# Another written-out order for a fused linear-attention and squared-ReLU kernel

## The chip, the cores and the metric

The kernel runs on one core of one Trainium2 chip. The metric is the device time of one execution in microseconds, as a median over runs. A smaller number is better.

## The reference

Two layers follow each other. The first is a linear attention with a decaying state, for 4 batches, 8 heads, 768 positions and a head width of 48; the second is a feed-forward block with a squared ReLU, on 3072 tokens of width 384 and a hidden width of 2048.

```python
for t in range(S):
    cur = einsum('bhd,bhe->bhde', u * k[t], v[t])
    y[t] = einsum('bhd,bhde->bhe', r[t], state + cur)
    state = w[None, :, :, None] * state + einsum('bhd,bhe->bhde', k[t], v[t])
x = y.transpose(0, 2, 1, 3).reshape(B * S, H * D)
h = np.maximum(x @ w_in, 0.0)
out = (h * h) @ w_out
```

Inputs and output are float32. TensorE works on bfloat16 copies of them.

## The kernel before

**Units.** The 768 positions are cut into 6 chunks of 128. A unit is one chunk of one batch, so there are 24 units; unit `i` belongs to chunk `i // 4` and batch `i % 4`. A unit's attention goes through these steps, each a Python function of the kernel:

- `load` brings the unit's k, r or v from memory (192 KB each, three DMAs per unit). `scale:i:1` multiplies k by a power of the decay, `scale:i:0` multiplies r, both on VectorE into the tile `rkw`. `cast_v` makes the bfloat16 copy of v on ScalarE.
- `turn` (TensorE transposes, for units 0 to 5, copied out of PSUM by ScalarE's `evict_rk`) or `turn_dma` (a DMA transpose on SyncE's queue, for units 6 to 23) gives `rkT`. `rk` multiplies its halves on VectorE.
- `at` (or `ats` for two units at once) computes the attention scores on TensorE; `mask` evicts them on VectorE in two halves (`mask:i:0`, `mask:i:1`) into `am`. `sums` computes the diagonal and the state's increment; `state_add`, `state_decay` (VectorE) and `state_cast` (ScalarE) carry the state on.
- `y_mm` computes the unit's y on TensorE; `diag_v` and `evict_y` on VectorE add the diagonal part and write `yb`. `x_turn` and `evict_x` (units 0 to 5) or a DMA transpose `x_dma` on SyncE's queue (units 6 to 23) give `xT`, the input of the feed-forward block.

**The feed-forward block.** `mm1:i:m:s` multiplies `xT` of `m` units (one at a time in the first two chunks, two at a time later) by a slice `s` of w_in. `relu` evicts it on ScalarE into `gr`; `square` makes `g` either on ScalarE (`...:1`) or on VectorE (`...:0`). `mm2:i:q` multiplies a quarter of the hidden width by w_out into a bank that stays open over q = 0 to 3; `evict_o` on ScalarE and `store` bring the result out. The last unit's product is done in two halves (`mm2_half`, `evict_half`, `store_half`).

**The order.** Nothing is left to a scheduler. The table `SCHEDULE` holds all words in one list, and each engine executes its own words in the list's order; the engines meet only through the waits that the data need. `load:3:kt:POOL` names the queue that issues a DMA (SyncE's or GpSimd's). The numbers behind `@` are the PSUM banks of the word, out of eight: a word that takes a bank waits until whoever read the bank's last content is done. `fill` is a matmul on constants whose result nobody reads; it stands only in the first part of the list.

```python
for word in SCHEDULE.split():
    times, _, word = word.rpartition("*")
    word, _, taken = word.partition("@")
    name, *args = word.split(":")
    for _ in range(int(times or 1)):
        given[:] = [int(x) for x in taken.split(",") if x]
        steps[name](*[value(x) for x in args])
```

In the profile's rows, lines of the kernel stand for these words: L232 `fill`, L236 `spread_log`, L287 `scale`, L301 `turn_dma`, L310 `turn`, L314 `evict_rk`, L319 `rk`, L327 `at`/`ats`, L339 `mask`, L347 and L352 `sums`, L361 `diag_v`, L390 and L396 `y_mm`, L405 `evict_y`, L414 `x_dma`, L420 `x_turn`, L424 `evict_x`, L434 `mm1`, L442 `relu`, L451 and L453 `square`, L460 `mm2`, L467 `evict_o`, L475 `mm2_half`.

## Time and profile before

| | us |
|---|---|
| median of 3 runs (lowest, highest) | 174.15 (173.06, 174.81) |
| the profiled execution | 172.5 |
| its span, from the first to the last instruction | 170.4 |
| TensorE busy in the span | 163.4 |
| VectorE busy | 137.0 |
| ScalarE busy | 120.9 |
| GpSimd busy | 30.5 |

The span is what the trace shows; 2.1 us of the profiled execution lie around it. That execution is 1.65 us shorter than the median of the runs without a profile, and the runs themselves lie 1.75 us apart. Busy time of TensorE contains the constant matmuls of `fill`, and its instructions are pipelined, so that the times of two neighbours overlap: the distance from one start to the next tells what a matmul costs.

### The profile page before, as it was taken

How to read it: one execution, taken by the hardware profiler on the slowest of the kernel's cores; microseconds unless marked ns; L12 is line 12 of the kernel's file. 1: busy time of each engine (PE TensorE's matmuls, PEld its weight loads, DVE VectorE, ACT ScalarE, POOL GpSimd, SP SyncE). 2: the span in 40 equal slices, each digit the busy share in tenths (PEclk: the TensorE clock that was granted, in tenths of full speed). 3: DMA queues.
4: the chain of work that ended last, by engine and by line, in shares of the span. 5: the costliest groups of instructions: out<-in, count | busy, mean ns of one | idle time of the engine just before them, and what ended most of it. 6: DMA issues, size and time to landing. Idle time of an engine off the chain costs nothing.

```text
span 170.4 us, 4781 instructions
## 1 busy us (share of the span) xinstructions
PE 163.4 (96%) x1917; PEld 129.9 (76%) x1917; DVE 137.0 (80%) x297; ACT 120.9 (71%) x253; POOL 30.5 (18%) x62
## 2 busy tenths in 40 slices
PE   3899999999999999999999999999999999999993
PEld 2467998778778786795796895896898776999662
DVE  5359969969998999799988979988999898664800
ACT  3355489997685988579499499599359985295830
POOL 7989540000000500001100001203000030030010
PEclk9999999999999999999999999999999999999999
DMA  6999999989999999998999994998989994150014
GB/s 115 188 220 211 221 248 244 227 155 129 187 159 187 209 237 133 192 207 131 250 203 116 200 217 81 251 192 176 252 100 212 197 159 139 27 162 0 4 63 167
DMA packets 94784, 28.83 MB, mean 169 GB/s; under 512 B 90665, under 2 KB 92714, under 8 KB 94762
## 3 DMA queue, kind: packets, MB, share of 16 engines
q1 hardware_dynamic: 90512, 19.08, 73.9%
q0 software_dynamic: 4224, 9.44, 21.4%
q8 instruction: 15, 0.25, 0.6%
q14 instruction: 7, 0.06, 0.2%
q10 hardware_dynamic: 26, 0.00, 0.0%
HBM read 20.45 MB, written 4.72 MB: 148 GB/s over the span
## 4 chain that ended last, share of the span: by engine, by line
PE 84%; DVE 6%; DMA 5%; issue 1%; ACT 1%; ACTq 1%; DVEq 0%
PE bank L434 35%; PE bank L460 31%; PE bank L327 4%; DMA xT<-yb 3%; PE bank L390 3%; DMA rkT<-rkw 2%; PE bank L352 2%; PE bank L232 2%; PE bank L396 2%; PE bank L310 2%; PE bank L475 2%; DVE am L339 1%; DVE rkw L287 1%; PE bank L347 1%; DVE g L453 1%
## 5 line engine op out<-in xcount | busy, mean ns | idle before, releaser
L442 ACT ACTIVATE gr<-bank 128x512 f32<-128x512 f32 x96 | 53.1, 603 | 27.3 <-PE bank L434 25.9
L434 PE MATMUL bank<-xT,w_in_q 128*128 128x128 bf16 (+1 forms) x768 | 70.8, 246 | 0.6 <-DMA xT<-yb 0.4
L460 PE MATMUL bank<-w_out_q,g 128*128 128x384 bf16 x368 | 68.1, 327 | 0.1
L434 PEld LDWEIGHTS <-w_in_q 128*128 128x128 bf16 x768 | 64.2, 113 | 3.4 <-DMA xT<-yb 0.5
L460 PEld LDWEIGHTS <-g 128*128 128x128 bf16 x368 | 33.7, 98 | 19.2 <-DVE g L453 0.6
L453 DVE TENSOR_TENSOR g<-gr 128x512 bf16<-128x512 f32 x49 | 32.4, 686 | 6.9 <-ACT gr L442 6.8
L494 POOL DMA_DIRECT2D out_dram<-osb x21 | 11.3, 543 | 129.4 <-ACT osb L467 118.7
L339 DVE TENSOR_TENSOR am<-bank,smask 128x512 bf16<-128x512 f32 x48 | 31.4, 685 | 2.9 <-PE bank L327 2.8
L451 ACT ACTIVATE g<-gr 128x512 bf16<-128x512 f32 x47 | 29.1, 638 | 0.6
L287 DVE TENSOR_TENSOR rkw<-ldk,wneg 128x384 bf16<-128x384 f32 x24 | 13.2, 553 | 4.8 <-ACT wneg L240 3.6
L381 ACT CAST stb<-st 64x192 bf16<-64x192 f32 x40 | 13.9, 348 | 2.6 <-DVE st L375 2.3
L361 DVE TENSOR_TENSOR dv<-vb,bank 128x384 f32<-128x384 bf16 x24 | 13.0, 550 | 2.4 <-PE bank L352 1.5
L405 DVE TENSOR_TENSOR yb<-bank,dv 128x384 bf16<-128x384 f32 x24 | 13.3, 555 | 1.3 <-PE bank L396 0.3
L287 DVE TENSOR_TENSOR rkw<-ldr,wpos 128x384 bf16<-128x384 f32 x24 | 13.1, 553 | 1.0 <-DMA ldr<-in_r_dram 0.8
L319 DVE TENSOR_TENSOR rk<-rkT 128x512 bf16<-128x512 bf16 x24 | 10.0, 420 | 3.8 <-ACT rkT L314 2.0
L467 ACT COPY osb<-bank 128x384 f32<-128x384 f32 x23 | 10.5, 483 | 2.7 <-PE bank L460 2.7
L291 ACT CAST vb<-ldv 128x384 bf16<-128x384 f32 x24 | 12.1, 512 | 0.4 <-DMA ldv<-in_v_dram 0.3
L371 DVE TENSOR_TENSOR st<-bank,st 64x192 f32<-64x192 f32 x32 | 11.2, 351 | 1.2 <-PE bank L352 0.9
L232 PE MATMUL bank<-warm 128*128 128x256 bf16 x39 | 9.2, 334 | 2.0 <-DVE warm L183 1.5
L314 ACT COPY rkT<-bank 128x512 bf16<-128x512 bf16 x12 | 6.9, 595 | 3.7 <-PE bank L310 3.6
L390 PEld LDWEIGHTS <-am 128*128 128x128 bf16 x192 | 7.9, 96 | 2.0 <-issue 0.7
L327 PEld LDWEIGHTS <-rkT 64*128 64x128 bf16 x192 | 5.5, 96 | 4.2 <-issue 3.9
(58 smaller groups left out, 112.2 us busy)
## 6 DMA issues: line engine op xcount, KB each, us to landing
ldk<-in_k_dram SPq DMA_DIRECT2D x22, 192.0 KB, 4.6
out_dram<-osb POOLq DMA_DIRECT2D x21, 192.0 KB, 3.3
ldr<-in_r_dram SPq DMA_DIRECT2D x20, 192.0 KB, 3.7
ldv<-in_v_dram SPq DMA_DIRECT2D x19, 192.0 KB, 4.3
w_in_q<-in_moe_w_in_dram POOLq DMA_DIRECT2D x4, 384.0 KB, 8.9
w_out_q<-in_moe_w_out_dram POOLq DMA_DIRECT2D x4, 384.0 KB, 10.7
ldv<-in_v_dram POOLq DMA_DIRECT2D x5, 192.0 KB, 9.0
ldr<-in_r_dram POOLq DMA_DIRECT2D x4, 192.0 KB, 8.2
```

Source lines behind the costliest of these rows:

```text
L232: nc.tensor.matmul(out=banks[given.pop(0)][:, :n], lhsT=warm[:, :128], rhs=warm[:, :n], start=True, stop=True)
L287: nc.vector.tensor_tensor(t["rkw"][:, x, :, :, :D], pair(src), pair(wx), ALU.mult)
L339: nc.vector.tensor_tensor(am, t["at"][o], smask.unsqueeze(1).to_broadcast([C, HP, C]), ALU.mult)
L361: nc.vector.tensor_tensor(t["dv"], t["vb"], t["d"].unsqueeze(2).to_broadcast([C, H, D]), ALU.mult)
L381: nc.scalar.copy(stb[b][sl, :, o * D : (o + 1) * D], st32[b][sl])
L390: nc.tensor.matmul(out=y[:, 2 * p + o, :], lhsT=t[f"am{o}"][:, p, :], rhs=t["vb"][:, 2 * p + o, :], start=(o == 0 and p == 0), stop=c == 0 ...
L405: nc.vector.tensor_tensor(t["yb"], t["y"], t["dv"].rearrange("p h d -> p (h d)"), ALU.add)
L434: nc.tensor.matmul(out=t["h", s][:, a], lhsT=turned, rhs=chunks[c]["xT"][:, n, b : b + m, :], start=(n == 0), stop=(n == NK - 1),)
L442: nc.scalar.activation(t["gr", s], t["h", s], AF.Relu)
L451: nc.scalar.activation(g, x, AF.Square)
L453: nc.vector.tensor_tensor(g, x, x, ALU.mult)
L460: nc.tensor.matmul(out=t["o"], lhsT=chunks[units[i][0]]["g"][:, f, units[i][1], :], rhs=w_out_q[f // 4][:, f % 4, :], start=(f == 0), stop ...
```

## The change

Only the table `SCHEDULE` changes. The words are the same but for two kinds: 37 `fill` instead of 39, and 55 of the 96 `square` words on ScalarE and 41 on VectorE, where it was 47 and 49. All loads and stores stay on the queue that issued them before, and GpSimd's words keep their order but for stores that change places among themselves; among SyncE's words some neighbours change places. The orders of TensorE, ScalarE and VectorE, and the PSUM banks, are new from beginning to end. The list's first lines and the piece around units 8 to 11 show the kind of difference:

```diff
-load:1:kt:SP load:1:rt:POOL fill@7 load:0:rt:SP 2*fill@7 load:1:vt:POOL fill@7 load:0:kt:SP 3*fill@7 load:2:kt:SP
-constants load:2:vt:SP load:2:rt:POOL spread_log@0 win:0:0 load:5:rt:SP load:0:vt:POOL fill@7
-power:1 spread_columns@1 power:0 scale:1:1 win:1:0 fill@7 scale:1:0 fill@7 turn:1:1@2 load:3:kt:POOL copy_columns
-scale:0:0 fill@0 load:5:kt:SP evict_rk:1:1 turn:1:0@3 u_columns turn:0:0@4 evict_rk:1:0 fill@2 win:2:0 fill@2
...
+load:1:kt:SP load:1:rt:POOL fill@7 load:0:rt:SP 2*fill@7 load:1:vt:POOL load:0:kt:SP load:2:kt:SP constants
+load:2:vt:SP load:2:rt:POOL spread_log@0 win:0:0 load:5:rt:SP load:0:vt:POOL fill@7 power:0 2*fill@7 power:1 fill@7
+scale:1:0 spread_columns@1 win:1:0 scale:1:1 load:3:kt:POOL scale:0:0 fill@0 turn:1:0@2 load:5:kt:SP scale:0:1
+turn:1:1@3 fill@0 evict_rk:1:1 3*fill@0 evict_rk:1:0 fill@0 turn:0:0@4 cast_v:1 rk:1 fill@2 copy_columns at:1@5,6
+u_columns fill@1 mask:1:0 turn:0:1@7 win:2:0 sums:1@0 scale:2:0 evict_rk:0:1 fill@1 load:3:rt:POOL 2*fill@5 mask:1:1
...
-mm1:8:2:5@6 evict_y:10 relu:8:2:6 load:12:vt:SP square:8:2:2:0 mm2:9:0@4 x_dma:10 relu:8:2:5 state_add:11 mm2:9:1
-square:8:2:5:1 state_add:10 mm2:8:0@3 cast_v:13 load:15:kt:SP evict_o:6 state_decay:10 load:15:rt:SP mm2:8:1
-relu:8:2:7 scale:14:1 load:16:kt:SP store:6:POOL evict_o:7 mm2:8:2 state_decay:8 rk:13 state_cast:8 store:4:POOL
-square:8:2:7:0 ats:12@6,2,5,0 store:5:POOL scale:14:0 mm2:9:2 mask:13:1 turn_dma:14 sums:13@7 mm1:10:2:0@1
...
+square:8:2:1:1 diag_v:10 y_mm:10@5 x_dma:11 relu:8:2:6 scale:14:1 mm2:9:0@2 square:8:2:4:1 evict_y:10 mm1:8:2:7@6
+scale:14:0 square:8:2:6:1 x_dma:10 square:8:2:2:0 mm2:8:0@5 relu:8:2:7 state_add:10 mm2:8:1 relu:8:2:5 load:15:kt:SP
+state_add:11 mm2:9:1 load:15:rt:SP square:8:2:5:1 evict_o:6 load:14:vt:SP rk:13 ats:12@6,0,1,4 evict_o:7 turn_dma:14
+cast_v:13 store:6:POOL mm2:8:2 mask:12:1 store:5:POOL sums:13@7 mask:13:1 mm1:10:2:0@3 store:4:POOL load:16:kt:SP
```

Three places are looked at more closely. The table is one line shorter now, so every line number behind it is smaller by one.

**VectorE, units 0 to 2, near the beginning.** The tiles `rkw_115`, `rkw_116` and `rkw_117` are those of units 0, 1 and 2, `am` are the masked scores of unit 1. Before:

```order
L319 TENSOR_TENSOR rk<-rkT 128x512
L287 TENSOR_TENSOR rkw_115<-ldk_101,wneg 128x8x48
L287 TENSOR_TENSOR rkw_117<-ldr_97,wpos 128x8x48
L339 TENSOR_TENSOR am_272<-bank_66,smask 128x512
L339 TENSOR_TENSOR am_278<-bank_67,smask 128x512
L287 TENSOR_TENSOR rkw_117<-ldk_103,wneg 128x8x48
L361 TENSOR_TENSOR dv<-vb,bank_68 128x384
```

Now:

```order
L318 TENSOR_TENSOR rk<-rkT 128x512
L247 COPY cols<-bank_62 128x8
L338 TENSOR_TENSOR am_251<-bank_66,smask 128x512
L286 TENSOR_TENSOR rkw_117<-ldr_97,wpos 128x8x48
L338 TENSOR_TENSOR am_276<-bank_67,smask 128x512
L286 TENSOR_TENSOR rkw_117<-ldk_103,wneg 128x8x48
L360 TENSOR_TENSOR dv<-vb,bank_61 128x384
```

The first `mask` of unit 1 has moved ahead of `scale:2:0`, which reads the loaded tile `ldr_97`; `scale:0:1` has moved ahead of `rk:1`, and the small copy `copy_columns` from ahead of it to behind it.

**VectorE, a little later, the last eviction of the three units that start the feed-forward block.** `yb` are the attention results of units 0 and 2, `rkw_118` is unit 3's tile. Before:

```order
L405 TENSOR_TENSOR yb<-bank_64,dv 128x384
L339 TENSOR_TENSOR am_418<-bank_61,smask 128x512
L361 TENSOR_TENSOR dv<-vb,bank_66 128x384
L287 TENSOR_TENSOR rkw_118<-ldk_104,wneg 128x8x48
L405 TENSOR_TENSOR yb<-bank_64,dv 128x384
```

Now:

```order
L404 TENSOR_TENSOR yb<-bank_63,dv 128x384
L338 TENSOR_TENSOR am_416<-bank_65,smask 128x512
L360 TENSOR_TENSOR dv<-vb,bank_66 128x384
L404 TENSOR_TENSOR yb<-bank_63,dv 128x384
L286 TENSOR_TENSOR rkw_118<-ldk_104,wneg 128x8x48
```

`scale:3:1` has moved from ahead of `evict_y:2` to behind it.

**SyncE's queue, units 8 to 11.** `rkw_119` and `rkw_120` are units 10 and 11, the two transposes of `yb` are those of units 9 and 8 in both orders, `ldr_95` is the load of unit 12. Before:

```order
L301 DMA_TRANSPOSE rkT<-rkw_119 128x8x128
L266 DMA ldr_95<-in_r_dram 128x8x48
L414 DMA_TRANSPOSE xT<-yb 128x3x128
L301 DMA_TRANSPOSE rkT<-rkw_120 128x8x128
L414 DMA_TRANSPOSE xT<-yb 128x3x128
```

Now:

```order
L265 DMA ldk_105<-in_k_dram 128x8x48
L265 DMA ldr_95<-in_r_dram 128x8x48
L300 DMA_TRANSPOSE rkT<-rkw_119 128x8x128
L300 DMA_TRANSPOSE rkT<-rkw_120 128x8x128
L413 DMA_TRANSPOSE xT<-yb 128x3x128 x2
```

The load of unit 12 stands ahead of the four transposes, and unit 11's transpose ahead of both transposes of `yb`.

More of the change, by code (lines that the diff above doesn't have):

```diff
@@ new lines @@
+mm1:1:1:2@4 square:1:1:1:0 evict_rk:3:1 state_add:2 turn:3:0@6 relu:2:1:0 mm1:2:1:2@0 evict_rk:3:0 state_add:0
+mm1:0:1:2@1 wout:3:0 relu:0:1:1 square:0:1:0:1 load:5:vt:POOL fill@3 square:0:1:1:0 at:3@5,6 square:2:1:0:1
+mm1:1:1:3@3 mask:3:0 cast_v:3 mm1:2:1:3@2 rk:3 relu:1:1:0 mask:3:1 sums:3@5 square:1:1:0:1 mm1:2:1:1@7 diag_v:3
+relu:1:1:3 mm1:0:1:3@6 relu:2:1:1 y_mm:3@3 relu:0:1:2 mm2:2:0@7 evict_y:3 relu:1:1:2 mm2:1:0@1 scale:4:0 relu:0:1:3
+square:2:1:1:0 state_cast:0 mm2:0:0@3 scale:4:1 x_turn:3@4 square:1:1:2:1 turn:4:0@6 state_add:3 mm2:0:1 evict_rk:4:0
@@ new lines @@
+sums:14@2 scale:17:0 relu:12:2:0 y_mm:14@5 state_decay:12 mm2:11:2 turn_dma:17 scale:19:1 square:12:2:0:1 diag_v:15
+mm1:12:2:6@1 state_cast:12 evict_y:15 mm2:13:0@6 load:17:vt:SP relu:12:2:2 diag_v:14 x_dma:15 mm1:12:2:4@3
+square:12:2:2:1 evict_y:14 relu:12:2:6 mm2:12:0@7 state_add:14 x_dma:14 square:12:2:6:1 mm2:12:1 state_decay:13 rk:17
+relu:12:2:4 mm2:11:3 scale:18:1 evict_o:10 load:19:vt:SP square:12:2:4:0 square:12:2:5:1 ats:16@5,1,2,3 load:19:rt:SP
+store:10:POOL cast_v:16 mm2:13:1 mask:16:0 load:18:vt:SP square:12:2:7:1 store:7:POOL mm2:12:2 scale:18:0
```

162 lines of the change are left out of this document (75 added, 87 removed).

## The prediction

> **What bounds the kernel now.** I read the page's busy shares first, then the chain that ended last, then the windows of ten microseconds, and then TensorE's timeline, because the shares already say where to look.
>
> ```profile
> PE 163.4 (96%) x1917; PEld 129.9 (76%) x1917; DVE 137.0 (80%) x297; ACT 120.9 (71%) x253; POOL 30.5 (18%) x62
> PE 84%; DVE 6%; DMA 5%; issue 1%; ACT 1%; ACTq 1%; DVEq 0%
> 10.00:20.00 10.00, 9.40 (x149) 7.77 (x146) 8.97 (x19) 4.34 (x9) 7.76 (x15) 1.00 1.20 221
> 50.00:60.00 10.00, 10.00 (x152) 8.26 (x151) 9.34 (x21) 7.71 (x18) 2.18 (x4) 1.00 0.92 176
> 70.00:80.00 10.00, 9.74 (x108) 8.10 (x107) 9.88 (x22) 7.64 (x16) 0.00 (x0) 1.00 1.19 190
> 80.00:90.00 10.00, 9.65 (x117) 7.93 (x116) 9.11 (x19) 7.48 (x17) 1.60 (x3) 1.00 1.12 210
> ```
>
> In the windows the columns after the stretch are its length and the busy time of PE, PEld, DVE, ACT and POOL, then granted clock, DMA share and GB/s. TensorE is busy without a break in most windows, and the chain runs on it for 84% of the span. A new order removes no matmul but two constant ones. What it can win is therefore only what TensorE loses now: the beginning, where it waits or runs constants, and the waits behind it. TensorE's own timeline sizes both.
>
> ```profile
> 1.46 1.67 PE L232 MATMUL bank<-warm 128*128 128x256 bf16 x7 [1.46 <-DVE warm L183]
> 9.01 0.85 PE L232 MATMUL bank<-warm 128*128 128x256 bf16 x3
> 13.29 0.60 PE L232 MATMUL bank<-warm 128*128 128x256 bf16 x4
> 20.51 2.17 PE L434 MATMUL bank<-xT,w_in_q 128*128 128x128 bf16 x36
> 65.03 4.25 PE L460 MATMUL bank<-w_out_q,g 128*128 128x384 bf16 x24
> 69.22 0.62 PE L327 MATMUL bank<-rkT 64*128 64x128 bf16 x16
> 69.81 1.48 PE L434 MATMUL bank<-xT,w_in_q 128*128 128x256 bf16 x12
> 71.50 0.82 PE L434 MATMUL bank<-xT,w_in_q 128*128 128x256 bf16 x6 [0.21 <-DVE am L339]
> 76.04 1.47 PE L434 MATMUL bank<-xT,w_in_q 128*128 128x256 bf16 x12
> 77.56 3.41 PE L460 MATMUL bank<-w_out_q,g 128*128 128x384 bf16 x20
> 82.22 0.33 PE L352 MATMUL bank<-vb,rkw 128*128 128x96 bf16 x4
> 82.90 4.12 PE L434 MATMUL bank<-xT,w_in_q 128*128 128x256 bf16 x36 [0.35 <-DMA xT<-yb]
> 164.79 2.80 PE L475 MATMUL bank<-w_out_q,g 128*128 128x256 bf16 x32
> ```
>
> From start to start, a full `mm2` word (4 matmuls) costs 0.65, an `mm1` word 0.67 (12 narrow matmuls) or 0.655 (6 wide ones). Behind 20.5 us I find four waits: 65.03 to 69.22 holds six `mm2` words of 0.65 and lasts 4.19, of which 0.1 goes with every change to L327, so 0.2 is lost; 69.81 to 71.50 holds two wide `mm1` words and loses 0.4; 76.04 to 77.56 the same two and loses 0.2; 82.22 to 82.90 holds a word of 0.17 and loses 0.5. **Together 1.3 us in 147.** The chain of waits says what was late:
>
> ```profile
> 65.08 4.25 DMA rkT<-rkw
> 69.36 0.42 DVE rk L319
> 70.75 0.70 DVE am L339
> 78.26 4.59 DMA xT<-yb
> ```
>
> Two DMA transposes on SyncE's queue: `turn_dma:11` landed at 69.33, VectorE stood before `rk:11`, its `mask` words came late, and the backlog delayed `evict_y:10` and with it `x_dma:10`, which landed at 82.85.
>
> **The beginning.** TensorE starts the first word of the gapless part at 20.51; the word after that, `mm1:2:1:0`, follows 0.67 later, at 21.18. In the new list the same words stand ahead of `mm1:2:1:0`, except one `turn` of 0.22 that now follows, so the time to beat is 20.96. VectorE sets the pace here:
>
> ```profile
> 9.79 0.55 DVE L287 TENSOR_TENSOR rkw<-ldk,wneg 128x384 bf16<-128x384 f32 x1
> 11.16 0.56 DVE L287 TENSOR_TENSOR rkw<-ldr,wpos 128x384 bf16<-128x384 f32 x1 [0.83 <-DMA ldr<-in_r_dram]
> 11.64 1.28 DVE L339 TENSOR_TENSOR am<-bank,smask 128x512 bf16<-128x512 f32 x2
> 18.99 0.55 DVE L287 TENSOR_TENSOR rkw<-ldk,wneg 128x384 bf16<-128x384 f32 x1
> 19.46 0.55 DVE L405 TENSOR_TENSOR yb<-bank,dv 128x384 bf16<-128x384 f32 x1
> 8.19 1.71 ACT L314 COPY rkT<-bank 128x512 bf16<-128x512 bf16 x3 [0.82 <-PE bank L310]
> ```
>
> VectorE stands 0.83 before `scale:2:0`, whose load lands then, with `mask:1:0` queued behind it. The new order lets the mask go first. That is not worth 0.83: ScalarE's first word is still `evict_rk:1:1`, but TensorE now makes the other half first, so ScalarE starts about 0.5 later than 8.19 (one constant more and the second `turn` before it), and `at:1` 0.35 later. The mask can start near 10.8 instead of 11.64. From there to `evict_y:2` VectorE's work is the same as before: `scale:2:0` is new in the stretch (0.47), and `scale:3:1` has left it (0.47 between 18.99 and 19.46). So `evict_y:2` is possible at 18.65, but now it follows directly on `diag_v:2`, `y_mm:2` has to wait for `mask:2:1`, and nothing covers that: I add 0.35 and put it at 19.0 against 19.46. **This term is -0.45.** Its bounds: -0.85 if the whole shift arrives, +0.4 if only ScalarE's lateness does. The new place of `copy_columns` lets GpSimd's `u_columns` end near 11.5; `sums:1` is hidden behind constants until about then, and its reader `diag_v:1` starts only near 13, so I cost it at nothing. Without that cover it is what `sums:1` moves, 0.8. GpSimd's next weight load leaves 1.6 us later, behind five that are still on their way; if its landing moved by all of this, one `mm1` word would wait 0.25. I take nothing. One `fill` is left behind 20.5: +0.1.
>
> The clock of the array counts here too: a constant matmul costs 0.21 from start to start at 9.01 and 0.11 at 13.29, at a granted clock of 1.00. The Trainium skill, "TensorE: Matmul & The Clock Gate", Part 1, says that the array starts at half clock and is let go only after a full window of activity, about 3.4 us, whose phase is free. The trace agrees with the two speeds and not with more. By that rule fewer early constants speak against the change; what this would cost is the second rival.
>
> **The middle.** Here the question is what is late next. Eight `square` words move to ScalarE:
>
> ```profile
> L453 DVE TENSOR_TENSOR g<-gr 128x512 bf16<-128x512 f32 x49 | 32.4, 686 | 6.9 <-ACT gr L442 6.8
> L451 ACT ACTIVATE g<-gr 128x512 bf16<-128x512 f32 x47 | 29.1, 638 | 0.6
> 59.99 2.23 SPq L301 DMA_TRANSPOSE rkT<-rkw  x1
> 62.94 2.04 SPq L414 DMA_TRANSPOSE xT<-yb  x1
> 65.08 1.25 SPq L301 DMA_TRANSPOSE rkT<-rkw  x1
> 66.43 1.63 SPq L414 DMA_TRANSPOSE xT<-yb  x1
> 74.97 1.24 SPq L301 DMA_TRANSPOSE rkT<-rkw  x1
> 78.26 2.76 SPq L414 DMA_TRANSPOSE xT<-yb  x1
> DMA to landing us min/median/max: 2.3/3.7/5.6
> DMA to landing us min/median/max: 3.2/4.3/5.2
> ```
>
> VectorE gives up 8 x 0.686 = 5.5 us and ScalarE takes 8 x 0.638 = 5.1 us; ScalarE has 49 us idle, VectorE is the fuller one in the windows above, so this is relief and costs nothing on the path. The last two rows are the landings of the `x_dma` (`xT`) and `turn_dma` (`rkT`) transposes. SyncE's issues follow each other almost without a gap, so a transpose leaves when the one ahead of it has.
>
> Units 8 to 11: unit 11's transpose no longer stands behind unit 12's load and unit 9's `x_dma`. VectorE finishes `scale:11:1` near 62.1, so `turn_dma:11` leaves at 62.2 instead of 65.08 and lands 4.25 to 5.2 later, 66.5 to 67.4; `ats:10` comes near 67.3, and `rk:11` now stands behind two masks and a `scale`, near 69.7. The waits of 0.2 and 0.4 go. Behind it `x_dma:9` and `x_dma:8` leave at 63.6 and 65; `x_dma:8` lands after 3.2 to 4.0 us (its own row to `mm1`, 66.43 to 69.81, held 3.25 of it), at 68.2 to 69.0, for an `mm1` near 69.2. I put 0.1 there.
>
> Units 10 and 11: the four DMAs `turn_dma:13` to `x_dma:10` took from 74.97 to 82.85, 7.9 us. In the new list `turn_dma:13` can leave near 73.15, so `x_dma:10` lands near 81.05, while its reader `mm1:10` comes near 80.55. It stands `mm2` x4, `ats` and `sums` behind it, 4 x 0.65 + 0.55 + 0.27 = 3.4 us of TensorE's work, where 4.1 us stood before. The wait stays: 0.4. For all pairs behind that I add 0.3, since `x_dma:16` too has 3.4 us of cover (before: 5.4 for the later of its pair) and `x_dma:21` 2.3 (3.2). The sum is 0.8 instead of 1.3: **-0.5**, with bounds from -1.3, none left, to +2.7, which is the first rival.
>
> **The end.** From 164.79 on TensorE runs the last two halves without a wait, and the new list ends with the same words; nothing.
>
> **The sum** is -0.45 + 0.1 - 0.5 = -0.85 us: a span of 169.55 instead of 170.4, an execution of 171.65 instead of 172.5. The profiled execution lies 1.65 below the median of the runs shown, 174.15, so I forecast a median of **173.3 us**, 0.5% faster. About 1% is what a measurement of this kernel can tell from no change.
>
> **Rivals.** First, the slower side: *the transposes come late.* The new list puts `x_dma` nearer to its reader at units 8 (3.8 us of TensorE's work instead of 4.45), 10 (3.4 instead of 4.1), 12 (3.8 instead of 4.5) and 16 (3.4 instead of 5.4), while loads fill the same queue. If each lands as `x_dma:10` did, 4.6 after its issue, these four places wait 0.8 + 1.2 + 0.8 + 1.2 = 4.0 us instead of 1.3: +2.7, and with the beginning's -0.35 the time is **176.5 us**. It decides from landings of about 4.2 us on. For it speaks the queue without gaps, against it that the median landing is 3.7 and that SyncE's queue is emptier near units 16 to 23.
>
> Second, *no change, the beginning is lost to a slow array*: if constants still cost 0.21 rather than 0.11 while the five attention words from `turn:2:0` to `at:2` run (0.22, 0.2, 0.22, 0.33 and 0.33 at the faster pace), these take twice their time, +1.3, which eats the gain: **174.6 us**. For it speaks that three constants instead of seven stand before the first wait, against it that TensorE is busy from 6.2 us on in both.
>
> Third, *more than that*: all four waits go (-1.3) and the whole shift of the beginning arrives (-0.85), +0.1 for the `fill`: -2.05, **172.1 us**, 1.2% faster. For it speaks that three of the four waits had one cause, against it the shorter covers.
>
> **How the numbers follow.** Forecast 0.45, transposes late 0.26, no change 0.13, more 0.16. Faster by over 1% is the third rival and a little of the forecast, 0.17; slower by over 1% is most of the first, 0.25; within 1% 0.58. The forecast's own range is 172.4 to 174.2; with the rivals on both sides the range is 171.6 to 176.6.
>
> **What would show it.** In the profile of the changed kernel the 36 narrow `mm1` words of the beginning's end should be under way by 20.5, VectorE should have no wait for `ldr` ahead of its first mask, `rk` should no longer wait 1 us for a transpose near 69, and the wait for `xT` near 80.5 should be there with 0 to 0.8 us. ScalarE should show 55 `square` words and no new wait of TensorE for `gr`. I am wrong if idle time of TensorE before L434 and `xT` sums to more than 2 us, if the constants still take 0.21 behind 13 us, or if waits appear for a PSUM bank that ScalarE reads late.

## The result, and the profile after

The changed kernel is slower: a median of 174.15 us (173.23 to 177.68, 20 runs) against 173.24 us (171.85 to 177.06, 20 runs) for the kernel before in the same comparison. The ratio is **1.0093, with a 95% interval of 1.0068 to 1.0117**. Ratios, here and below, leave out the long runs (over 1.5% above the fastest run of the same kernel), so they differ from the quotient of the medians, which is 1.0053 here. That the new median is the same number as the old one of the table above is chance: that one was the median of three runs only. Its profiled execution took 173.78 us with a span of 172.0 (before: 172.5 and 170.4).

The page of the changed kernel, the busy shares, the two kinds of `square`, and the group of `rk`:

```profile
PE 163.1 (95%) x1915; PEld 129.8 (75%) x1915; DVE 132.4 (77%) x289; ACT 125.2 (73%) x261; POOL 30.6 (18%) x62
L452 DVE TENSOR_TENSOR g<-gr 128x512 bf16<-128x512 f32 x41 | 27.5, 688 | 12.1 <-ACT gr L441 11.9
L450 ACT ACTIVATE g<-gr 128x512 bf16<-128x512 f32 x55 | 34.1, 636 | 0.5
L318 DVE TENSOR_TENSOR rk<-rkT 128x512 bf16<-128x512 bf16 x24 | 10.1, 420 | 4.7 <-DMA rkT<-rkw 3.6
```

VectorE gave up 4.6 us in all and ScalarE took 4.3, a little less than the 5.5 and 5.1 worked out for the squares alone. TensorE does 0.3 us less work in a span that is 1.6 us longer: all of the loss is idle time of TensorE. Its timeline holds four waits behind 60 us that the new order brings or keeps (the last column is the idle time ahead of a row, and what ended it):

```profile
67.56 0.40 PE L326 MATMUL bank<-rkT 64*128 64x128 bf16 x8
68.41 0.40 PE L326 MATMUL bank<-rkT 64*128 64x128 bf16 x8 [0.45 <-DMA rkT<-rkw]
71.66 1.47 PE L433 MATMUL bank<-xT,w_in_q 128*128 128x256 bf16 x12
73.89 0.36 PE L389 MATMUL bank<-vb,am 128*128 128x48 bf16 x8 [0.76 <-ACT gr L441]
105.80 0.82 PE L459 MATMUL bank<-w_out_q,g 128*128 128x384 bf16 x4
107.00 1.31 PE L459 MATMUL bank<-w_out_q,g 128*128 128x384 bf16 x7 [0.38 <-DVE g L452]
121.60 0.81 PE L459 MATMUL bank<-w_out_q,g 128*128 128x384 bf16 x4
123.01 0.82 PE L433 MATMUL bank<-xT,w_in_q 128*128 128x256 bf16 x6 [0.60 <-DVE yb L404]
```

Counted from start to start against the durations used in the prediction, they lose 0.65, 0.92, 0.55 and 0.76 us. With small ones beside them the waits behind 60 us are 3.2 us; before, the same count gives 1.5. From 20.5 to 60 us the kernel before loses 0.65 and the changed one 0.83, with one `fill` in it. The beginning gains 0.3 (see below). Together this is the whole of the loss: -0.3 + 0.2 + 1.7 = 1.6 us, by which the last matmul ends later, at 169.21 instead of 167.59.

**The one mechanism in four places.** The queues and the other two engines show what ended each wait. SyncE's queue in the changed kernel, near the four places:

```profile
58.30 1.93 SPq L265 DMA_DIRECT2D ldr<-in_r_dram  x1
60.33 4.47 SPq L300 DMA_TRANSPOSE rkT<-rkw  x2
64.89 3.94 SPq L413 DMA_TRANSPOSE xT<-yb  x2
68.93 0.54 SPq L265 DMA_DIRECT2D ldv<-in_v_dram  x1
100.80 2.67 SPq L300 DMA_TRANSPOSE rkT<-rkw  x1
113.94 0.69 SPq L265 DMA_DIRECT2D ldr<-in_r_dram  x1
117.62 2.50 SPq L413 DMA_TRANSPOSE xT<-yb  x2
```

The tile view of its `rkT` between 60 and 64 us splits the second row into its two issues, of 3.12 and 1.25 us, and gives the time to landing of the later one:

```profile
L300 SPq DMA_TRANSPOSE rkT<-rkw x2: 1249/2183/3117, 60.3 to 63.6; - x2
DMA to landing us min/median/max: 4.8/4.8/4.8
```

In the kernel before, `x_dma:16` left ahead of `x_dma:17`, in this row:

```profile
114.19 1.88 SPq L414 DMA_TRANSPOSE xT<-yb  x1
```

And ScalarE and VectorE of the changed kernel at the second and the third place:

```profile
72.09 0.51 ACT L290 CAST vb<-ldv 128x384 bf16<-128x384 f32 x1 [4.27 <-DMA ldv<-in_v_dram]
73.25 1.57 ACT L441 ACTIVATE gr<-bank 128x512 f32<-128x512 f32 x3
105.44 0.43 DVE L318 TENSOR_TENSOR rk<-rkT 128x512 bf16<-128x512 bf16 x1 [0.79 <-DMA rkT<-rkw]
106.26 0.68 DVE L452 TENSOR_TENSOR g<-gr 128x512 bf16<-128x512 f32 x1
```

- *68.41, inside `ats:10`.* `turn_dma:10` occupied SyncE from 60.33 for 3.12 us (before: 2.23 for the same transpose), so `turn_dma:11` left at 63.55 and landed 4.8 later, at 68.36. The second half of `ats:10` starts at 68.41.
- *73.89, `y_mm:11`.* It waits for no attention value but for its PSUM bank. ScalarE stands 4.27 us at `cast_v:10` for v of unit 10, issued at 68.93 and landed at 72.07. The `relu` that frees the bank is queued behind that cast.
- *107.00, `mm2:12:2`.* VectorE stands 0.79 at `rk:17` for a transpose that left at 100.80 and landed at 105.42; the `square` at 106.26, which the matmul reads, is queued behind it.
- *123.01, `mm1:16:2:1`.* SyncE issues nothing between 114.63 and 117.62: `x_dma:17` stands first in its queue and waits for `evict_y:17`. `x_dma:16` behind it left at 118.86 and landed 4.0 later, at 122.88, while before it left at 114.19. The releaser in the row, `yb`, is not the cause: `evict_y:18` stands behind this matmul in the list.

So each time a transfer lands late. At 68.41 and 123.01 TensorE itself meets the landing; at 73.89 and 107.00 another engine stands there, and TensorE waits for what is queued behind on that engine. To compare kernels I add up, over all 85 transfers on SyncE's queue that land behind 40 us, how long the first reader's engine stood for the landing (landing less the end of the word ahead of the reader, where positive). This sum of **stands** is 3.5 us before and **13.3 us** after. It counts late landings, not lost time: the stand of 2.46 us at `rk:15` (92.85) has no wait of TensorE behind it.

### The profile page after: what moved, and what is told of

Same layout as the page of the kernel before. It is cut to its first block, busy times and chain, and to the rows that moved or that the text cites. A ratio compares the mean times of both kernels' runs of the same rounds, so it can differ in the third digit from the quotient of the medians.

```text
span 172.0 us, 4773 instructions
## 1 busy us (share of the span) xinstructions
PE 163.1 (95%) x1915; PEld 129.8 (75%) x1915; DVE 132.4 (77%) x289; ACT 125.2 (73%) x261; POOL 30.6 (18%) x62
## 5 line engine op out<-in xcount | busy, mean ns | idle before, releaser
L433 PE MATMUL bank<-xT,w_in_q 128*128 128x128 bf16 (+1 forms) x768 | 72.3, 246 | 0.6 <-DVE yb L404 0.6
L441 ACT ACTIVATE gr<-bank 128x512 f32<-128x512 f32 x96 | 54.5, 601 | 20.8 <-PE bank L433 20.1
L452 DVE TENSOR_TENSOR g<-gr 128x512 bf16<-128x512 f32 x41 | 27.5, 688 | 12.1 <-ACT gr L441 11.9
L450 ACT ACTIVATE g<-gr 128x512 bf16<-128x512 f32 x55 | 34.1, 636 | 0.5
L286 DVE TENSOR_TENSOR rkw<-ldr,wpos 128x384 bf16<-128x384 f32 x24 | 13.3, 553 | 4.9 <-ACT wpos L239 3.6
L286 DVE TENSOR_TENSOR rkw<-ldk,wneg 128x384 bf16<-128x384 f32 x24 | 13.3, 553 | 1.4 <-DMA ldk<-in_k_dram 1.3
L466 ACT COPY osb<-bank 128x384 f32<-128x384 f32 x23 | 11.0, 484 | 2.1 <-PE bank L459 2.1
L231 PE MATMUL bank<-warm 128*128 128x256 bf16 x37 | 8.6, 336 | 1.5 <-DVE warm L182 1.5
L389 PE MATMUL bank<-vb,am 128*128 128x48 bf16 x192 | 8.7, 183 | 0.8 <-ACT gr L441 0.8
```

The costliest lines, as they stand in the source:

```text
L286: nc.vector.tensor_tensor(t["rkw"][:, x, :, :, :D], pair(src), pair(wx), ALU.mult)
L389: nc.tensor.matmul(out=y[:, 2 * p + o, :], lhsT=t[f"am{o}"][:, p, :], rhs=t["vb"][:, 2 * p + o, :], start=(o == 0 and p == 0), stop=c == 0 ...
L433: nc.tensor.matmul(out=t["h", s][:, a], lhsT=turned, rhs=chunks[c]["xT"][:, n, b : b + m, :], start=(n == 0), stop=(n == NK - 1),)
L441: nc.scalar.activation(t["gr", s], t["h", s], AF.Relu)
L450: nc.scalar.activation(g, x, AF.Square)
L452: nc.vector.tensor_tensor(g, x, x, ALU.mult)
```

## The experiments

All times are medians; ratios are against the kernel before on the same chip. "End" is the end of the last matmul in the trace (before: 167.59, changed: 169.21). The table's length differs between the kernels, and the line numbers with it, by up to three.

### Is the slowdown there again, and does one word carry it?

The changed kernel once more, unaltered:

> The changed kernel, unaltered, once more. Theory A (late landings at four fixed places): the first trace of it shows four waits of TensorE that the kernel before lacks, inside ats:10 near 67.6 (0.6 us), ahead of y_mm:11 near 73.1 (0.9), ahead of mm2:12:2 near 106.6 (0.6) and ahead of mm1:16:2:1 near 122.3 (0.8). They should come again at the same four places, each within 0.4 us of its size, and the ratio should be 1.007 to 1.012. Theory B (no places, only scatter: words without slack wait wherever a landing happens to be late): at least two of the four are gone and others of 0.5 us or more stand elsewhere, with the same ratio.

173.99 us against 172.62, ratio 1.0069 [1.0026, 1.0112]. Its profiled execution was the one of 330.19 us that the last section tells of, so whether the four waits come again is left to `six_moves`, below.

`cast_v:10`, the word on which ScalarE stands 4.27 us, goes behind the `relu` that frees the bank:

```diff
-cast_v:10 rk:11 ... relu:8:2:0 scale:13:1
+rk:11 ... relu:8:2:0 cast_v:10 scale:13:1
```

> The changed kernel with cast_v:10 moved behind relu:8:2:0 on ScalarE, where the kernel before has it. Theory A: ScalarE no longer stands about 4 us before the load of v, relu:8:2:3 empties its bank near 71.6, TensorE's wait ahead of y_mm:11 goes, and the time falls by 0.9 us: ratio about 1.004. Rival C (SyncE's queue is the bound, not the word): what TensorE gains there it waits for at x_dma:10 or turn_dma:12 some us later, and the ratio stays at 1.008 or more.

174.02 us, ratio 1.0063 [1.0022, 1.0103]. The wait at `y_mm:11` is gone, that at `mm2:12:2` is not there either, and the end stays at 169.20: 0.59 before `mm1:7:1:0` and 1.06 at 87.6 are new. The first of these, at 62.0, stands ahead of the moved word, where the two kernels have the same words; the move did not make it, so one execution differs from another by as much as a wait.

The same for all four places:

```diff
-ats:10 rk:10 ... mask:11:1 mm2:7:2      +rk:10 ... mm2:7:2 ats:10 mask:11:1
-rk:17 relu:12:2:4 square:12:2:4:0       +relu:12:2:4 square:12:2:4:0 rk:17
-square:14:2:0:0 ... evict_y:16 ... x_dma:16   +evict_y:16 x_dma:16 square:14:2:0:0
```

> The changed kernel with four moves, one for each wait: cast_v:10 behind relu:8:2:0; ats:10 behind two mm2 words (mm2:7:2); rk:17 behind square:12:2:4:0 on VectorE; evict_y:16 ahead of square:14:2:0:0 and x_dma:16 with it, ahead of x_dma:17. Theory A: all four waits go, 0.7 + 0.9 + 0.6 + 0.8 = 3.0 us, TensorE ends near 166.2 instead of 169.2, ratio to the kernel before about 0.992. Rival C: each time gained is given back at the next landing; ratio 1.002 or more.

173.85 us, ratio 1.0059 [1.0025, 1.0092]. All four waits are gone, 2.9 us, and the end is 169.21, as without the moves. Two new waits, of 0.92 and 2.07 us from start to start, have taken their place. TensorE's timeline, and the tile view of `xT` at the transpose concerned, show them:

```profile
71.67 0.26 PE L347 MATMUL bank<-uwb,rk 128*128 128x8 bf16 x4 [0.76 <-DVE rk L319]
83.82 2.16 PE L434 MATMUL bank<-xT,w_in_q 128*128 128x256 bf16 x18 [1.90 <-DMA xT<-yb]
L414 SPq DMA_TRANSPOSE xT<-yb x1: 3298/3298/3298, 78.1 to 78.1; - x1
DMA to landing us min/median/max: 5.7/5.7/5.7
```

The first is made by the moves: `sums:11` waits for `rk:11`, which VectorE has behind two masks of the later `ats:10`. The second is `mm1:10:2:0`, which waits for `x_dma:10`. TensorE was ready for it 0.66 us earlier than in the changed kernel (81.75 instead of 82.41). The larger part is that the transpose landed later, at 83.77 instead of 82.32, though it had left earlier, at 78.11 instead of 79.52: its issue alone occupied SyncE for 3.3 us, and it landed 5.7 after its start.

### The beginning alone

The kernel before with the changed words up to about 22 us. The bank numbers of the old rest do not suit this beginning, so that some of the first products are overwritten before they are read.

> The kernel before with the change's beginning only: all words up to turn:3:0 and relu:2:1:0 (about 22 us, constants included) in the new order, the rest in the old one. Theory A: the beginning is not where the time went; TensorE's last matmul comes 0.3 us earlier than in the kernel before, ratio 0.996 to 1.000. Rival D (the fewer early constants keep the array slow, or GpSimd's loads come later and delay the first matmul words): ratio 1.005 or more.

173.16 us, ratio 1.0020 [0.9978, 1.0062]: no gain and no loss that can be told from nothing.

### Engines' order or queues' order

Both mixtures: the changed order of TensorE, ScalarE and VectorE with the old order of SyncE's and GpSimd's words, and the reverse.

```diff
 (queues_old, SyncE)
-load:12:kt load:12:rt turn_dma:10 turn_dma:11 x_dma:9 x_dma:8
+load:12:kt turn_dma:10 load:12:rt x_dma:9 turn_dma:11 x_dma:8
 (queues_new: the kernel before, with the - row in place of the + row)
```

> The change's order of TensorE, ScalarE and VectorE, with the words of SyncE and GpSimd in the order of the kernel before. Theory E (the new order of the queues lost the time: turn_dma:11 and x_dma:16 leave where the landing is too late): ratio 0.998 or less, since the beginning's 0.3 us stays. Theory F (the new order of the three engines lost it: its words have no slack behind a landing): ratio 1.007 or more, with three or four waits of TensorE of 0.5 us or more, as in each trace of the change so far.

> The other way round: the order of TensorE, ScalarE and VectorE of the kernel before, with the words of SyncE and GpSimd in the change's order. Theory E: ratio 1.007 or more. Theory F: 0.997 to 1.003. If both mixed kernels are slow, the two parts belong together, and neither alone is at fault.

179.60 us, ratio 1.0391 [1.034, 1.0441], with 8.3 us of waits behind 60 us; and 174.53 us, ratio 1.0100 [1.0069, 1.0132]. (The latter's profiled execution was its fastest run, 172.66 us, so its trace cannot carry the 1%.) The order of the queues and that of the engines belong together; neither half of the change is good by itself.

### Fewer transfers

Both kernels without the loads of units 12 to 23 (these units work on the data of earlier ones):

```diff
         x = tiles[i][name] = x[i % len(x)]
+        if i >= 12:
+            return
```

> The changed kernel without the loads of units 12 to 23 (36 loads of 192 KB; these units are computed from data that lies in the buffers), so that SyncE's queue has some 45 us less to move behind 57 us. Theory C (the transfers are the second bound; what TensorE loses it loses at landings): its waits behind 60 us fall from 3.0 us to under 0.6, TensorE ends near 166.7, the ratio to the kernel before is near 0.985. Rival G (the waits come from the order of the engines themselves, such as a bank that ScalarE reads late): they stay, ratio 1.004 or more.

> The kernel before without the same 36 loads. Theory C: its 1.5 us of waits behind 60 us go as well, ratio to the kernel before 0.989 to 0.994, and the change, without these loads, is then the faster one by the 0.3 us of its beginning. Rival G: the kernel before keeps its lead of 1 us or more over the change with the loads gone in both.

171.50 us, ratio 0.9960 [0.9934, 0.9986], and 171.52 us, ratio 0.9934 [0.9905, 0.9964]. The two medians are equal. By the ratios 0.26% is left of the difference, with an uncertainty of about 0.4% (worked out from the two intervals), so most of it is gone, but not surely all. The 0.985 that was forecast for the changed kernel was not reached. The scatter is smaller too: the runs lie within 171.17 and 172.14, and 170.94 and 172.18, while the kernel before beside them ran from 171.05 to 173.38, with two more runs at 174.18 and 175.54. The windows from 60 to 130 us, of the kernel before, the changed one, and the changed one without these loads, in this order (the last two columns are the busy share of the DMA engines and GB/s):

```profile
60.00:130.00 70.00, 69.38 (x786) 55.76 (x784) 63.36 (x134) 53.28 (x113) 4.81 (x9) 1.00 1.10 185
```

```profile
60.00:130.00 70.00, 67.81 (x770) 53.92 (x768) 59.94 (x128) 52.58 (x111) 4.82 (x9) 1.00 1.04 181
```

```profile
60.00:130.00 70.00, 69.69 (x791) 56.55 (x790) 61.27 (x132) 54.87 (x117) 4.83 (x9) 1.00 0.46 102
```

With all loads the DMA engines are full for these 70 us (a share of 1.04 to 1.10), without the late ones half empty; TensorE's busy time goes from 67.81 to 69.69 of 70, and the stands, over the fewer transfers that are left, fall from 13.3 to 4.1 us (old order: 3.5 to 1.0). The transposes land sooner as well. The tile views of `rkT`, of the changed kernel and of the same without these loads, count the transposes whose landing they give (`turn_dma:10` of the changed kernel, with 7.2 us, is not among them):

```profile
DMA to landing us min/median/max: 3.6/4.8/5.7
DMA to landing us min/median/max: 3.0/3.3/5.2
```

The loads that are left out were also issues on SyncE's queue, so this does not tell a full queue from full DMA engines.

### Loads on the other queue

If only SyncE's queue were the limit, moving 14 loads of v (units 10 to 23) to GpSimd's should help.

```diff
-load:10:vt:SP ... load:23:vt:SP
+load:10:vt:POOL ... load:23:vt:POOL
```

> The changed kernel with the loads of v of units 10 to 23 (14 loads) issued by GpSimd at the same places of the list, so that SyncE has 14 issues less and the DMA engines move the same bytes. Theory H (SyncE's one queue is what the landings wait for): the transposes leave 0.6 us earlier for each load taken away, TensorE's waits behind 60 us fall from 3.0 to under 1.5, ratio 1.000 or less. Theory I (the DMA engines are full, their share reads 0.95 to 1.3 in every window from 10 to 140 us): the transposes leave earlier and land as late as before, ratio 1.005 to 1.012.

> The kernel before with the same 14 loads of v on GpSimd's queue. Theory H: its 1.5 us of waits behind 60 us fall by half or more, ratio 0.993 to 0.997. Theory I: ratio 0.998 or more; over 1.005 if a load that overtakes a transpose takes its bandwidth.

187.09 us, ratio 1.0764 [1.0715, 1.0814], and 188.72 us, ratio 1.0901 [1.0853, 1.0950]: much slower for both orders, which neither theory had forecast. GpSimd's queue, TensorE's timeline, and the window from 60 to 80 us (its third column from the end is the granted clock) of the first:

```profile
59.53 3.54 POOL L267 DMA_DIRECT2D ldv<-in_v_dram  x4
73.39 0.61 PE L328 MATMUL bank<-rkT 64*128 64x128 bf16 x8 [5.43 <-DMA rkT<-rkw]
60.00:80.00 20.00, 14.24 (x155) 10.06 (x153) 12.47 (x27) 9.36 (x21) 3.08 (x4) 0.83 1.16 174
```

Four loads leave at once, and the transpose `turn_dma:10` behind them in time, on the other queue, lands at 73.34 instead of 67.50; `ats:10` waits 5.4 us. For some 5 us behind this wait the matmuls also run at half pace (the granted clock of the window is 0.83), so it costs more than itself. Three of the four loads left 8 to 15 us earlier than they do on SyncE's queue: the run moves them in time as well as to another queue. So it shows that loads on one queue delay a transpose on the other, behind the issuing; it does not show what SyncE's queue alone costs. The Trainium skill, "DMA: Bandwidth & Descriptors", section "Issuing engines are not separate DMA queues", says that transfers of all issuing engines run on the same 16 DMA engines and interleave there; these rows agree.

### More moves in both orders

The changed kernel with the four moves and eight others; then with six of those eight alone. Most put a cast, an `rk` or a `scale` word one or two places further from its landing, or another word ahead of it (`mask:12:0` ahead of `scale:15:0`, `mm2:9:2` ahead of `mm1:10:2:0`); `rk:11`, whose transpose is there in time, goes three places forward:

```diff
 (both kernels)
-cast_v:15 ... relu:12:2:1                +relu:12:2:1 cast_v:15
-rk:15, scale:13:1, scale:22:0            +each of them one or two words later
-scale:15:0 ... mask:12:0                 +mask:12:0 scale:15:0
-mm1:10:2:0 ... mm2:9:2                   +mm2:9:2 mm1:10:2:0
 (more_moves: these, the four moves, and)
-relu:8:2:0 cast_v:10 ... relu:8:2:4      +relu:8:2:0 relu:8:2:4 cast_v:10
-mask:11:1 mask:11:0 scale:12:0 ... rk:11 +rk:11 mask:11:1 mask:11:0 scale:12:0
```

> The changed kernel with the four moves and eight more, each of which lets another word of the same engine go ahead of one that stood before a landing in the traces: on ScalarE cast_v:10 and cast_v:15 one word later, on VectorE rk:11 three places earlier (its transpose is there), mask:12:0 ahead of scale:15:0, rk:15 two later, scale:13:1 and scale:22:0 one later, on TensorE mm2:9:2 ahead of mm1:10:2:0. Theory J (words without slack at the landings are the cause, and four were too few): engines stand before landings for under 5 us in all instead of 13, TensorE's waits behind 60 us fall to 1.5 us or less, ratio 0.997 to 1.001. Rival C: other landings become the last, waits stay at 2.5 us or more, ratio 1.004 or more.

> The changed kernel without the first four moves and with six of the others alone: cast_v:15, rk:15, scale:13:1 and scale:22:0 later, mask:12:0 ahead of scale:15:0, mm2:9:2 ahead of mm1:10:2:0. None of the six stands at one of the four waits of TensorE in the first trace. Theory J in its strong form (every engine's stand before a landing counts, since it makes the next DMAs late): a third to a half of the loss goes, ratio 1.003 to 1.006. In its weak form (only those count that reach TensorE): the four waits stay, ratio 1.006 to 1.010.

`more_moves`: 173.70 us, ratio 1.0016 [0.9974, 1.0058], from 171.69 to 175.18; in its trace the stands are 2.4 us and the waits behind 60 us 1.5. That execution was the fastest of the twelve, 171.69 us, so the trace is a favourable one, and the medians alone lie 0.5% apart. `six_moves`: 174.06 us, ratio 1.0063 [1.0027, 1.0099]. Its timeline shows three of the four waits again, at the same words and of the same sizes:

```profile
68.50 0.40 PE L327 MATMUL bank<-rkT 64*128 64x128 bf16 x8 [0.50 <-DMA rkT<-rkw]
73.97 0.36 PE L390 MATMUL bank<-vb,am 128*128 128x48 bf16 x8 [0.75 <-ACT gr L442]
123.10 0.82 PE L434 MATMUL bank<-xT,w_in_q 128*128 128x256 bf16 x6 [0.58 <-DMA xT<-yb]
```

These three come with the order and not with one execution, and the last one is now put down to the transpose. The fourth, at `mm2:12:2`, is not in this trace.

In the kernel before I then moved three words away from their landings, and, in another kernel, four words of it as close to theirs as the changed order has them:

```diff
 (old_moves)
-rk:11 ... scale:12:1          +scale:12:1 rk:11
-scale:15:1 ... mask:12:0      +mask:12:0 scale:15:1
-rk:15 ... scale:16:0          +scale:16:0 rk:15
 (tight_old)
-relu:8:2:0 cast_v:10          +cast_v:10 relu:8:2:0
-mm2:6:3 ... ats:10            +ats:10 mm2:6:3
-state_add:12 ... rk:15        +rk:15 state_add:12
-x_dma:16 ... x_dma:17         +x_dma:17 x_dma:16
```

> The kernel before with three such moves on VectorE: rk:11 behind scale:12:1, mask:12:0 ahead of scale:15:1, rk:15 behind scale:16:0. Theory J: of its 1.5 us of waits behind 60 us about 0.8 go (ats:10 to x_dma:10), ratio 0.994 to 0.997. Rival C: given back, 0.999 or more.

> The kernel before, with four words put as close to their landings as the change has them: cast_v:10 ahead of relu:8:2:0 on ScalarE, ats:10 one mm2 word earlier on TensorE, rk:15 ahead of state_add:12 on VectorE, x_dma:16 behind x_dma:17 on SyncE. Theory J (words without slack at the landings are the cause): waits of TensorE inside ats:10, ahead of a word whose bank relu:8:2:0 empties late, and ahead of mm1:16:2:1 appear, 1.5 us more in all, ratio 1.005 to 1.010. Rival C (the pace of the transfers sets the time, wherever TensorE stands): ratio 1.002 or less.

`old_moves`: 172.93 us, ratio 1.0002 [0.9966, 1.0038], nothing. `tight_old`: 173.14 us, ratio 1.0039 [1.0004, 1.0074]: slower, but not where I had expected it; the wait was one of 2.0 us ahead of `mm1:10:2:0`, for `x_dma:10`. The places forecast for it are missed; that words closer to landings cost time holds, barely.

### Fewer transposes by DMA

If the DMA engines are the second bound, fewer transfers should help even where they cost TensorE work. `x_dma` of units 10 and 16 become a transpose on TensorE (0.17 each) with a copy on ScalarE, in `old_moves` with two choices of the bank, and in `more_moves`:

```diff
 (old_turns, on old_moves)
-mm2:9:0 x_dma:10 ... mm2:9:1            +mm2:9:0 ... mm2:9:1 x_turn:10@3 square:8:2:5:1 evict_x:10
-x_dma:16 sums:17                        +sums:17 x_turn:16@0 evict_x:16
 (old_turns_b)
-x_turn:10@3                             +x_turn:10@6
 (new_turns: the same two units, on more_moves, banks 6 and 5)
```

> The kernel before with the three moves of rk:11, mask:12:0 and rk:15, and with the transposes of units 10 and 16 from yb to xT on TensorE (x_turn and evict_x) instead of SyncE's queue. TensorE gets 2 x 0.17 us more, the DMA engines two transposes less, and no mm1 word waits for x_dma:10. If the transfers are the second bound, what lands behind them comes about 1 us earlier and the scatter of the runs shrinks: ratio 0.994 to 0.998. If not, the 0.34 us are lost: 1.001 to 1.004.

> The kernel of the run before this one (three moves, x_turn and evict_x for units 10 and 16 in the kernel before), with x_turn:10 on bank 6 instead of bank 3: in the trace mm2:8:0, the next word of TensorE, waited 0.73 us for bank 3 until evict_x:10 had read it. If the transfers are the second bound, that wait goes and what the two transposes free is seen: ratio 0.994 to 0.998, scatter of the runs within 1.5 us. If what is gained is lost elsewhere: 1.000 or more.

> The changed kernel with its eleven moves and, as well, x_turn and evict_x for units 10 and 16 in place of two transposes on SyncE's queue (banks 6 and 5). The eleven moves gave 1.0016. If the transfers are the second bound, waits of TensorE behind 60 us fall under 0.7 us and the ratio is 0.994 to 0.998; if the moves have already taken all that can be had, the 0.34 us of the two words are lost and it is 1.001 to 1.004.

`old_turns`: 172.58 us, ratio 1.0004 [0.9977, 1.0032]. Its bank 3 was a bad choice: the next taker, `mm2:8:0`, waits for ScalarE's copy. TensorE's timeline of `old_turns` has the first row, that of `old_turns_b` the two others:

```profile
79.17 1.14 PE L460 MATMUL bank<-w_out_q,g 128*128 128x384 bf16 x6 [0.57 <-ACT xT L424]
```

```profile
78.23 0.33 PE L420 MATMUL bank<-identb,yb 128*128 128x128 bf16 x3
78.40 2.11 PE L460 MATMUL bank<-w_out_q,g 128*128 128x384 bf16 x12
```

With bank 6 the wait is gone: **`old_turns_b` runs 171.74 us (171.22 to 172.85), ratio 0.9962 [0.9936, 0.9988], faster than the kernel before** and so than the changed one, which did not run beside it. Stands 0.9, waits behind 60 us 0.7. `new_turns` runs 173.27 us, ratio 1.0049 [1.0012, 1.0086]: its trace has 1.8 us of stands and 1.75 of waits, of which three small ones (0.25, 0.28, 0.38) stand in `more_moves` too. The new order did not reach the old one this way.

Last, the changed beginning in front of `old_turns_b`, with three bank numbers altered to fit:

> The kernel of the run before (three moves, units 10 and 16 turned on TensorE, 0.9962), with the change's beginning: all words up to 22 us in the change's order, constants included, three bank numbers altered where the two parts meet. Its runs lie within 1.7 us, so a term of 0.3 us can be seen. If the beginning is worth what the traces show (mm1:2:1:0 0.3 us earlier against the words left), TensorE ends near 166.8 and the ratio is 0.993 to 0.996. If it is worth nothing, since the pace of the array comes up at another time in each execution, 0.996 to 0.998. If the fewer constants cost something: over 0.998.

172.06 us, ratio 0.9972 [0.9935, 1.0010], no better than without it. The beginning is 0.6 us earlier in its trace (compared with `old_turns_b`), and TensorE's and VectorE's timelines show it handed back at a landing:

```profile
111.61 0.81 PE L434 MATMUL bank<-xT,w_in_q 128*128 128x256 bf16 x6 [0.85 <-DVE st L371]
110.36 0.56 DVE L287 TENSOR_TENSOR rkw<-ldr,wpos 128x384 bf16<-128x384 f32 x1 [0.53 <-DMA ldr<-in_r_dram]
```

`scale:19:0` stands 0.53 for its load, `state_add:16` behind it empties its bank late, and `mm1:14:2:3` waits.

## Why the prediction was wrong, step by step

The forecast was 173.3 us and 0.5% faster; it is 174.15 and 0.9% slower, on the wrong side of zero, just within the 1% that the text calls no change. That 174.15 lies inside the forecast's own range of 172.4 to 174.2 is luck: the offset, too large by 0.9 us, hid half of an error of 1.8 (below).

**The beginning, -0.45 with +0.1 for the `fill`: about right in size.** `mm1:2:1:0` starts at 20.64; the time to beat was 20.96, so it gained 0.32 where 0.35 were forecast. VectorE's first row has the mask at its place, and TensorE's rows the `mm1` words and the pace of the constants:

```profile
11.06 0.69 DVE L338 TENSOR_TENSOR am<-bank,smask 128x512 bf16<-128x512 f32 x1 [0.71 <-PE bank L326]
19.91 1.56 PE L433 MATMUL bank<-xT,w_in_q 128*128 128x128 bf16 x24
14.88 0.72 PE L231 MATMUL bank<-warm 128*128 128x256 bf16 x5
```

The mask starts at 11.06 (forecast 10.8) and no longer waits for `ldr`; `evict_y:2` came at 19.11 (forecast 19.0). What I had not seen is how little such a gain counts. In the nine traces that share the changed words up to here, `mm1:2:1:0` starts anywhere from 20.18 to 20.64; in the eight with the old words, from 20.12 to 20.97 (less the `turn`). The means are 20.47 and 20.72: a gain of 0.25, smaller than either spread, so the closeness of 0.32 to 0.35 is in part luck. The moment at which constants go from 0.21 to 0.11 also lies anywhere from 10 to 13 us; that it alone makes the spread is not shown. And `new_start` shows a gain of 0.6 spent at the next late landing.

**The middle, -0.5: this step failed.** The waits behind 60 us grew by 1.7 us instead of shrinking by 0.5. Three terms were wrong, the first in its sign:

1. *Unit 11's transpose.* "VectorE finishes `scale:11:1` near 62.1, so `turn_dma:11` leaves at 62.2." VectorE was done in time. But SyncE had issued the load of unit 12 at 58.30 for 1.93 us and then `turn_dma:10` for 3.12 us; the transpose left at 63.55. The prediction states that "a transpose leaves when the one ahead of it has", and then took the leaving time from VectorE instead of walking the new queue with its own issue times. It also says that unit 11's transpose no longer stands behind unit 12's load; in the new queue that load stands ahead of all four transposes. It landed at 68.36 instead of 66.5 to 67.4: a wait of 0.65 where none was forecast. The part behind was right: `rk:11` came at 70.52 without a wait. Of the waits that were to go, the 0.2 did not belong to this transpose: it lies between two `mm2` words, at 66.51, where a `square` of VectorE ends it, and `ats:10` of the kernel before has no wait for the landing at 69.33.
2. *Only transposes and their own readers were followed.* The 0.92 ahead of `y_mm:11` comes from a load of v, through a cast and a bank, and the 0.55 at `mm2:12:2` through a `square` behind `rk:17`. Neither is in the sum: I had looked at where each landing is read, not at who stands behind the reader on its engine.
3. *"For all pairs behind that I add 0.3".* `x_dma:16` was named, with its cover of 3.4 us instead of 5.4, and alone cost 0.76. `x_dma:10`, put at 0.4, cost nothing, by luck: it landed at 82.32, 1.3 later than forecast, for a reader at 82.4, since TensorE itself was late by then.

**The squares: as said in number.** 55 on ScalarE and relief for VectorE. That they cost nothing on the path is argued: no run moves them back alone. **The end: as said**, no wait.

**The offset, +1.65, was too large.** It rested on a median of three runs. Over 20 runs the kernel before lies 0.74 above its profiled execution. The forecast relative to the kernel before is what counts, and that was -0.85 us where +0.9 came by the medians and +1.6 in the profiled executions.

**What was to show it.** The signs named beforehand were half the right ones: no wait of `rk` near 69 and no wait for `xT` near 80.5 of more than 0.8 both came true, and idle time ahead of `mm1` for `xT` stayed at 0.76, below the 2 us that I had named. The one that was hit is the last, a wait for a PSUM bank that ScalarE reads late, at 73.89; the same row is the new wait of TensorE for `gr` that ought not to be there.

**The rivals.** The first, transposes that come late, had the chance of 0.26 and came nearest: waits at landings, and +1.6 at the end of the last matmul where it priced +2.35. But its condition did not hold. It asked for `x_dma` landings of 4.2 us or more at units 8, 10, 12 and 16; they took 2.3, 2.8, 2.3 and 4.0. Only unit 16 waited, since its transpose left late, and the rest of the loss came through `turn_dma`, a load, a cast and an `rk`. The second, the slow array, did not happen: constants cost 0.11 at 14.88, and the loss lies behind 60 us. The third did not happen.

**What carries the loss.** Shown: in the profiled execution it is idle time behind landings (the four rows, three of them again in `six_moves`), and without the late loads the medians of the two orders are equal (171.50 and 171.52, ratios 0.26% apart with intervals that overlap). Two runs support it more weakly: putting the kernel before's words closer to landings made it slower by 0.39%, with an interval that begins at 0.04% and a wait at another place (`tight_old`), and taking two transfers out of it made it faster by 0.38% (`old_turns_b`; `new_start`, with the same two taken out, has 0.28% and an interval that reaches 1.0010). The reading that fits most of it, argued and not shown: until about 140 us the DMA engines are as full as TensorE (a share of 0.94 to 1.27 in every window of 10 us from 10 to 140 us), so no order can bring the landings forward as a whole; an order that meets them later loses nothing, one that meets them 0.5 to 4 us earlier stands. It agrees with `four_moves`, where the transposes left earlier and landed no sooner, `x_dma:10` even 1.45 later. But late landings alone do not set the time: in the traces of `cast_later` and `four_moves` the idle time of the engines that ends with a landing, behind 40 us, is 6.7 and 6.9 us instead of the changed kernel's 12.7, and the time is the same. Not shown: what still holds `new_turns` at 1.0049 when its stands are down to 1.8 us (of the 1.18 us by which its profiled span is longer than that of the kernel before, 0.70 lie behind the last matmul, ahead of the end of the last store), and whether the loss of the changed kernel is split over the four places in other executions as in the profiled one.

## What to carry to other kernels

When a matmul-bound kernel's DMA engines are also near a share of 1, an order must be costed at the landings: for each transfer take the new queue, walk its issues with their own durations, and compare the landing with the word ahead of its first reader, loads and casts as well as transposes; then ask who stands behind that reader on its engine and whose PSUM bank it frees. A wait removed at one place can come back at the next: `four_moves` took away 2.9 us of waits and met 3.0 us of new ones. Fewer transfers are worth a trial even where they cost TensorE work: in the kernel before, two more transposes of 0.17 us in place of two transfers gave 0.9962, where three moves of words had given 1.0002. That is no rule: in the changed kernel the moves alone gave 1.0016, and with the same two transposes 1.0049.

## What the runs showed of the hardware beyond that

**An execution on a half-speed array to the end.** One run of the unaltered changed kernel took 330.19 us, and it was the profiled one. The busy shares of its page:

```profile
PE 321.7 (98%) x1915; PEld 204.5 (62%) x1915; DVE 134.5 (41%) x289; ACT 128.6 (39%) x261; POOL 30.7 (9%) x62
```

Its first three constants, at 1.46 us, take 0.11 to 0.12 from start to start; after an idle stretch they take 0.22 from 6.27 us on, and later matmuls run at that pace to the end, with TensorE busy 98%. The windows show a granted clock of 1.00, but this trace holds no record of the clock, so that figure says nothing. The Trainium skill, "TensorE: Matmul & The Clock Gate", Part 1, has the array let go after a full window of activity; that did not happen here in 320 us. It was one of twelve executions in that comparison; the others took 172.5 to 175.5 us. The kernel before had two far-off executions as well, of 918.75 and 190.25 us, in the comparisons of `old_turns_b` and `new_start`; neither was profiled.

**Issuing is not free.** One DMA transpose occupied SyncE for 1.2 to 3.3 us (up to 4.1 in `v_loads_gpsimd_new`), and the same `turn_dma:10` for 2.23 in one order and 3.12 in the other; from issue to landing they took 2.3 to 5.6 us in the kernel before, up to 7.2 in the changed one (`turn_dma:10`, 60.33 to 67.50), and 12.7 beside the four loads of `v_loads_gpsimd_new`. On a full set of DMA engines both numbers are those of the moment, and an estimate to half a microsecond, as the prediction made it, is finer than they allow.

**A late landing can cost more than its wait.** In the profiled execution of `new_beginning`, `mm1:10:2:0` waited 1.9 us for its `xT` and started at 84.07. Here is the window behind it:

```profile
84.20:87.60 3.40, 3.40 (x17) 2.43 (x17) 2.19 (x5) 1.71 (x3) 0.00 (x0) 0.50 1.32 204
```

The granted clock is 0.50, and the wide `mm1` matmuls take 0.21 from start to start instead of 0.11, so the wait cost another 1.7 us. Waits of 2.0 and 2.1 us at the same word, in `tight_old` and `four_moves`, were not followed by this.
